# Regrouping the weight loads of a decode kernel: wo by eight heads, w2 whole, the last K ahead of the last three V, w1's last rows dealt anew

## The chip, the cores and the metric

The kernel runs on one core of one Trainium2 chip. The metric is the device time of one execution in microseconds (us). A run of a kernel is several such executions on one chip, and they are timed in rounds against the kernel before on the same chip. The time is some 1.8 us longer than the span that the profile shows.

## The reference

```python
B, D, H, Dh, F = 4, 640, 32, 192, 1536         # bf16, one new token for each of 4 sequences
xn = layernorm(x)
q  = (xn @ wq)                                 # wq: 640 x 6144, 32 heads of 192
k, v = k_cache[:, :, -2048:], v_cache[:, :, -2048:]   # a window of the 8192 cached keys
o  = softmax(q k^T / sqrt(192)) v              # a head of its own for each query head
A  = o.reshape(4, 6144) @ wo                   # wo: 6144 x 640
Bf = (silu(xn @ w1) * (xn @ w3)) @ w2          # w1, w3: 640 x 1536; w2: 1536 x 640
out = x + A + Bf
```

For each head 3 MB of K and 3 MB of V come from memory and are used once. With the weights that makes 223 MB in one execution, against little arithmetic.

## The kernel before

Nearly all loads are issued by one engine (SP) into one queue (q1, 222.96 MB), and SP issues a load when its buffer is free: for a K buffer it waited 316.2 us in all, 30 times, for the `mult` that frees it. Time inside the program is counted in slots of a quarter of a head: `add(slot, phase, function, ...)` puts a piece of work into a slot, and `NU - 6` is a slot near the end.

A head's attention: `mult` (DVE) multiplies K by the broadcast query, `adder` (PE) sums over the 192 elements, a short softmax chain follows, and `pv` (PE) multiplies by V. `ge_sum` sums a head's result into `po`. When a group of HG heads is complete, `ge_turn` scales and transposes it to `oT`, and `ge_proj` multiplies it by the group's rows of wo into `acc`.

```python
def load_k(h):
    kt = kpool.tile([P, NJ, Dh], BF16, tag="kt")            # 2 buffers; the V pool has 3
    nc.sync.dma_start(out=..., in_=k_win[:, h]...)          # 24,576 B a partition
def wo_load(hg):                                            # HG = 4: eight loads of 768 rows
    wo_t = wopool.tile([P, RPP * D], BF16, tag="wo")        # RPP = 6 rows a partition
    nc.sync.dma_start(out=wo_t[:], in_=A_wo[hg * QW:(hg + 1) * QW, :].rearrange("(p i) n -> p (i n)", i=RPP))
...
# w1, 640 rows: 512 rows as four a partition, 64 rows as half a row a partition (128 partitions),
# and the last 64 rows on three DMA engines, four partitions each
def w1_load():
    nc.sync.dma_start(out=wt[:, 0:FM], in_=w[0:KM * P, :].rearrange("(p kc) n -> p (kc n)", kc=KM))
    nc.sync.dma_start(out=wt[:, FM:FH], in_=w[KM * P:LB, :].rearrange("r (h n) -> (r h) n", h=2))
def w1_low(n):
    if n < 2:        # two loads of 12 partitions, two rows each
        nc.sync.dma_start(out=we[n * CT:n * CT + LP, :], in_=w[...].rearrange("(i e s) n -> e i (s n)", e=LE, s=2))
    elif n == 2:     # one load of 12 partitions, one row each
    ...              # and one of 12 partitions, a third of a row each
...
for h in range(H - 2, H):                                   # the end of the queue
    add(NU - 6, 0, load_v, h)
add(NU - 6, 0, w2_load, 0)                                  # w2 rows 0-3 of 12 a partition
add(NU - 6, 0, w2_load, 1)                                  # rows 4-7
add(NU - 6, 0, wo_load, NG - 2)
add(NU - 6, 0, wo_load, NG - 1)
add(NU - 6, 0, w2_load, 2)                                  # rows 8-10
add(NU - 6, 0, w2_load, 3)                                  # row 11
```

Why three engines take the last 64 rows of w1: in the packet records of before the 15 instruction fetches (16,384 B each) go round eight other DMA engines, hit seven of them twice and make the engine hit 1.4 us late each time, so the kernel before loads three of the remaining ones a little more. These three are called the low engines below; that is only a name.

## Time and profile before

| | before |
|---|---|
| time, median of 3 (range) | 525.66 us (525.56 to 526.65) |
| span of the profiled execution | 523.80 us |
| last byte of the loads lands | 520.49 |
| last matmul ends | 521.09 |
| share of the span in which the DMA engines carry loads | 99.2% |

The middle three rows divide the end of the span into three parts: what the loads set (520.49), what must run behind the last byte (0.60), and what ends the program (2.71). A change of the loads acts on the first part, a change of the order on the second. A wait of PE in mid-kernel is in none of them: before the matmuls of `adder` it waited 137.5 us in all for DVE, and the loads still fill 99.2% of the span. The landing times are read from the trace's packet records, which give start, duration and size of every packet. They name no engine: where a text below speaks of one, its packets were followed from the end of one to the start of the next. The lines of the profile itself are in the prediction.

### The profile page before, as it was taken

To read this page: it belongs to the slowest core of one execution; us is meant where nothing else is said; L and a number is where in the kernel's file an instruction comes from. 1 tells how busy PE (TensorE), PEld (TensorE's weight loads), DVE (VectorE), ACT (ScalarE), POOL (GpSimd) and SP (SyncE) were. 2 spreads that over 40 slices of the span, in tenths; PEclk is the share of its full clock that TensorE was granted. 3 is DMA by queue.
4 is the path that set the end of the run, shared out by engine and by line. 5 is a ranking of instruction groups with operands and counts; after the bars stand their busy time and mean duration, and the time that the engine had idled before them with its cause. 6 is when DMAs were issued, how large, how long until landed. Compare 5 with 4: busy or idle time off the path is not lost.

```text
span 523.8 us, 4820 instructions
## 1 busy us (share of the span) xinstructions
PE 361.8 (69%) x2336; PEld 75.9 (14%) x1643; DVE 340.9 (65%) x413; ACT 55.8 (11%) x176; POOL 5.6 (1%) x12
## 2 busy tenths in 40 slices
PE   0965866887668776667547768586686876675685
PEld 0100111121111111111111111111111111111122
DVE  3268853687656767577646877466667766667671
ACT  2111111111001110101100111001101110011111
POOL 4000000000000000000000000000000000000000
PEclk9979886898878998789997988889878898889988
DMA  9999999999999999999999999999999999999996
GB/s 389 422 443 425 433 431 432 428 433 432 430 435 428 437 418 446 424 437 426 434 434 429 432 434 429 435 427 435 425 437 434 427 437 431 430 434 425 441 418 275
DMA packets 11904, 223.26 MB, mean 426 GB/s; under 512 B 1332, under 2 KB 1608, under 8 KB 3052
## 3 DMA queue, kind: packets, MB, share of 16 engines
q1 hardware_dynamic: 11868, 222.96, 99.2%
q8 instruction: 15, 0.25, 0.2%
q14 instruction: 5, 0.04, 0.0%
q10 hardware_dynamic: 16, 0.01, 0.0%
HBM read 222.96 MB, written 0.01 MB: 426 GB/s over the span
## 4 chain that ended last, share of the span: by engine, by line
DMA 60%; PE 20%; DVE 15%; ACT 3%; issue 1%; SPq 1%
DMA kt<-in_A_k_cache_dram 44%; PE ps L288 11%; DMA w<-in_B_w_dram 11%; DVE pr L277 10%; DMA vt<-in_A_v_cache_dram 5%; PE po L361 4%; PE qps L243 3%; DVE sc L296 2%; ACT ex L324 1%; DVE z L332 1%; DMA x_sb<-in_A_x_dram 1%; PE mt L318 1%; ACT L324 0%; ACT negm L321 0%; PE mt L305 0%
## 5 line engine op out<-in xcount | busy, mean ns | idle before, releaser
L288 PE MATMUL ps<-pr,idb 128*128 128x512 bf16 x768 | 214.7, 422 | 137.6 <-DVE pr L277 137.5
L277 DVE TENSOR_TENSOR pr<-kt,qbc 128x3072 bf16<-128x3072 bf16 x128 | 223.5, 1746 | 104.0 <-DMA kt<-in_A_k_cache_dram 104.0
L296 DVE TENSOR_REDUCE sc<-ps 128x16 f32<-128x512 f32 x128 | 87.1, 681 | 2.7 <-PE ps L288 2.6
L340 PE MATMUL o_ps<-vt,z 128*8 128x384 bf16 x1024 | 60.5, 380 | 0.2 <-DVE z L332 0.2
L361 PE MATMUL po<-o_sb,sel_w 128*32 128x192 f32 x128 | 49.2, 518 | 0.6 <-ACT o_sb L343 0.6
L340 PEld LDWEIGHTS <-z 128*8 128x8 bf16 x1024 | 26.2, 95 | 98.8 <-issue 89.2
L332 DVE TENSOR_TENSOR z<-ex,mask_b 128x256 bf16<-128x256 bf16 x32 | 13.5, 423 | 38.6 <-ACT ex L324 38.6
L343 ACT COPY o_sb<-o_ps 128x384 f32<-128x384 f32 x32 | 15.3, 478 | 196.9 <-PE o_ps L340 196.9
L313 ACT ACTIVATE gneg<-gmax 1x128 f32<-1x128 f32 x32 | 9.8, 308 | 162.8 <-DVE gmax L310 162.8
L305 PEld LDWEIGHTS mt<-idf,lmax 128*1 128x1 f32 x32 | 3.2, 101 | 127.5 <-issue 125.5
L361 PEld LDWEIGHTS po<-o_sb,sel_w 128*32 128x32 f32 x128 | 13.8, 130 | 29.4 <-issue 27.9
L288 PEld LDWEIGHTS <-idb 128*128 128x128 bf16 x124 | 12.0, 97 | 39.3 <-issue 32.8
L318 PEld LDWEIGHTS mt<-ones_ff,gneg 1*128 1x128 f32 x64 | 9.6, 186 | 47.1 <-issue 43.7
L243 PE MATMUL qps<-wt,xnT 128*128 128x512 bf16 x59 | 14.9, 412 | 0.1
L318 PE MATMUL mt<-ones_ff,gneg 1*128 1x1 f32 x64 | 12.3, 259 | 0.7 <-ACT gneg L313 0.7
L321 ACT COPY negm<-mt 128x1 f32<-128x1 f32 x32 | 5.1, 159 | 70.4 <-PE mt L318 70.4
L310 DVE TENSOR_REDUCE gmax<-mt 1x4 f32<-1x128 f32 x32 | 8.8, 274 | 5.8 <-PE mt L305 5.8
L348 PEld LDWEIGHTS po<-rsum,tot_w 128*32 128x32 f32 x64 | 4.4, 108 | 51.5 <-ACT ex L324 35.4
L249 DVE CAST qbc<-qps 128x512 bf16<-128x512 f32 x6 | 3.8, 684 | 11.7 <-PE qps L243 11.7
L324 ACT ACTIVATE ex<-sc,negm 128x64 bf16<-128x64 f32 x32 | 11.1, 348 | 1.0
L305 PE MATMUL mt<-idf,lmax 128*1 128x128 f32 x32 | 10.9, 340 | 0.0
L199 PE MATMUL xnT_ps<-idb,xn 4*128 4x4 bf16 x5 | 0.4, 178 | 13.4 <-DVE xn L194 13.4
(74 smaller groups left out, 84.4 us busy)
## 6 DMA issues: line engine op xcount, KB each, us to landing
kt<-in_A_k_cache_dram SPq DMA_DIRECT2D x32, 3072.0 KB, 19.1
vt<-in_A_v_cache_dram SPq DMA_DIRECT2D x32, 3072.0 KB, 25.5
wo_t<-in_A_wo_dram SPq DMA_DIRECT2D x8, 960.0 KB, 20.7
wt<-in_A_wq_dram SPq DMA_DIRECT2D x2, 3072.0 KB
w<-in_B_w_dram SPq DMA_DIRECT2D x1, 1920.0 KB
wt<-in_A_wq_dram SPq DMA_DIRECT2D x1, 1536.0 KB, 19.5
w<-in_B_w_dram SPq DMA_DIRECT2D x1, 1536.0 KB
w<-in_B_w_dram SPq DMA_DIRECT2D x2, 640.0 KB
```

Source lines behind the costliest of these rows:

```text
L243: nc.tensor.matmul(qp[:], lhsT=xnT[:, kc].rearrange("p a b -> p (a b)"), rhs=wq_rows[kc][:, (c0 + i) * QC:(c0 + i + 1) * QC], start=(kc == ...
L277: nc.vector.tensor_tensor(out=pr[:], in0=kts[h][:, g * JQ:(g + 1) * JQ, :], in1=qbc[:, h * Dh:(h + 1) * Dh].unsqueeze(1).to_broadcast([P, ...
L288: nc.tensor.matmul(ps[:], lhsT=idb[:], rhs=pr[:, :, kk * DD:(kk + 1) * DD], start=(kk == 0), stop=(kk == NK - 1))
L296: nc.vector.tensor_reduce(out=scs[h][:, g * JQ:(g + 1) * JQ], in_=pss.pop(u)[:], axis=AX.X, op=ALU.add)
L305: nc.tensor.transpose(out=mt[0:1, 0:P], in_=chs[h][0][:], identity=idf[:])
L313: nc.scalar.activation(out=gneg[:], in_=gmax[:].unsqueeze(1).to_broadcast([1, PB, B]), func=ACTF.Copy, scale=-SCALE)
L318: nc.tensor.matmul(mt[:, P:P + 1], lhsT=gneg[:].rearrange("o p b -> o (p b)"), rhs=ones_ff[:], start=True, stop=True)
L324: nc.scalar.activation(out=ex[:], in_=scs.pop(h)[:], func=ACTF.Exp, bias=negm[:, 0:1], scale=SCALE, accum_out=rsum[:])
L332: nc.vector.tensor_tensor(out=z[:], in0=ex[:].unsqueeze(2).to_broadcast([P, NJ, B]), in1=mask_b[:].unsqueeze(1).to_broadcast([P, NJ, B]), ...
L340: nc.tensor.matmul(o_ps[c * CT:c * CT + 2 * B, :], lhsT=z[:, 2 * jj:2 * jj + 2, :], rhs=vt[:, 2 * jj:2 * jj + 2, :], start=(jj < 4), stop= ...
L343: nc.scalar.copy(out=o_sb[:], in_=o_ps[:])
L361: nc.tensor.matmul(po[sl, 0:Dh], lhsT=sel_w[:, par].rearrange("p a b -> p (a b)"), rhs=o_sb[:, par * Dh:(par + 1) * Dh].rearrange("p (r i) ...
```

## The change

The intent: fewer and larger packets (wo in four loads instead of eight, w2 in one instead of four), the attention of the last heads out of the way of the last loads (K of the last head ahead of the last three V), and a deal of w1 in which each of the 16 engines has one packet less and the three low engines more.

```diff
-    HG: int = 4,
+    HG: int = 8,
+    FG: int = 4,
...
-    wopool = ctx.enter_context(tc.tile_pool(name="wo", bufs=2))
+    wopool = ctx.enter_context(tc.tile_pool(name="wo", bufs=1))
...
     def load_k(h):
-        kt = kpool.tile([P, NJ, Dh], BF16, tag="kt")
+        kt = (kpool if h < H - 1 else vpool).tile([P, NJ, Dh], BF16, tag="kt" if h < H - 1 else "vt", name="kt")
...
-    KM, PH, LE, LI = KC - 1, P // 2, 3, 4
+    KM, LE, LI, LS = KC - 1, 3, 4, 3
+    LP, LF = LE * LI, CT + LE * LI
+    PH = D - KM * P - 2 * LP * LS        # 56 rows, so 112 half rows
...
     def ge_turn(hg):
-        nc.vector.tensor_scalar_mul(out=og[:]..., in0=po[:, 0:Dh], scalar1=rts.pop(hg)[:, 0:1])
+        nc.vector.tensor_tensor(out=og[:], in0=po_v, in1=rts.pop(hg)[:]....to_broadcast([P, RPP, HB, RW]), op=ALU.mult)
...
-        nc.sync.dma_start(out=wt[:, FM:FH], in_=w[KM * P:LB, :].rearrange("r (h n) -> (r h) n", h=2))
+        nc.sync.dma_start(out=wt[0:2 * PH, FM:], in_=B_w1[KM * P:LB, :].rearrange("r (h n) -> (r h) n", h=2))
...
     def w1_low(n):
-        if n < 2: ...                    # four loads, 12 partitions each
+        b0 = LB + n * LS * LP            # two loads, 12 partitions of three rows each
+        nc.sync.dma_start(out=ffn["w1e"][n * CT:n * CT + LP].rearrange("p s n -> p (s n)"), in_=B_w1[b0:b0 + LS * LP, :]...)
...
-    ends = {H - 2: (NU - 1, NU), H - 1: (NU + 3, NU + 4)}
+    ends = {H - 3: (NU - 1, NU), H - 2: (NU + 2, NU + 3), H - 1: (NU + 4, NU + 5)}
+    early = {H - 1: (NU - 10, -1)}
...
+    WOC = [0, RPP - 5, RPP - 2, RPP]     # RPP is 12 now: rows 0-6, 7-9, 10-11
     for h in range(H - 2, H):
         add(NU - 6, 0, load_v, h)
-    add(NU - 6, 0, w2_load, 0)           # and the other five loads shown above
...
+    add(NU - 6, 0, w2_load)
+    for i0, i1 in zip(WOC, WOC[1:]):
+        add(NU - 6, 0, wo_load, NG - 1, i0, i1)
+        add(e, 6, ge_proj, NG - 1, i0, i1, True)
+    add(e - 1, 8, ffn_out)
```

More of the change, by code (lines that the diff above doesn't have):

```diff
@@ L87 @@
     CT = 32
+    HB = HG * CT // P
     QW = HG * Dh
     RPP = QW // P
+    RW = Dh // RPP
     NU = H * GQ
@@ L95 @@
     assert JQ * DD == 512 and JQ % 2 == 0 and 2 * Dh <= 512 and 2 * N0 == D and N0 <= 512
-    assert (H * Dh) % QC == 0 and NQ % 6 == 0 and QW % P == 0 and Dh == CT * RPP and P == HG * CT and F == HG * CT * FC
-    assert 2 * H * Dh <= NJ * Dh and KBUFS == 2 and VBUFS == 3
+    assert (H * Dh) % QC == 0 and NQ % 6 == 0 and QW % P == 0 and Dh == RW * RPP and CT == HB * RW and P == FG * CT and F == FG * CT * FC
+    assert 2 * H * Dh <= NJ * Dh and KBUFS == 2 and VBUFS == 3 and HB * (Dh + 1) <= 512 and H // HG > 1
     nc.at_finalize(keep_loaded_weights)
@@ L127, in load_k, with load_v, wo_load @@
         kts[h] = kt
-    def load_v(h, n=1):
-        vt = vpool.tile([P, NJ, Dh], BF16, tag="vt")
-        for j in range(0, NJ, NJ // n):
-            nc.sync.dma_start(out=vt[:, j:j + NJ // n].rearrange("q j d -> q (j d)"),
-                              in_=v_win[:, h].rearrange("b (p j) d -> p b j d", p=PB)[:, :, j:j + NJ // n].rearrange("p b j d -> p b (j d)"))
-        vts[h] = vt
-    def wo_load(hg):
-        wo_t = wopool.tile([P, RPP * D], BF16, tag="wo")
-        nc.sync.dma_start(out=wo_t[:], in_=A_wo[hg * QW:(hg + 1) * QW, :].rearrange("(p i) n -> p (i n)", i=RPP))
-        wos[hg] = wo_t
+    def load_v(h):
+        vt = (vpool if h < H - 1 else kpool).tile([P, NJ, Dh], BF16, tag="vt" if h < H - 1 else "kt", name="vt")
+        nc.sync.dma_start(out=vt[:].rearrange("q j d -> q (j d)"),
+                          in_=v_win[:, h].rearrange("b (p j) d -> p b (j d)", p=PB))
+        vts[h] = vt
+    def wo_load(hg, i0=0, i1=RPP):
+        if i0 == 0:
+            wos[hg] = wopool.tile([P, RPP * D], BF16, tag="wo", name="wo_t")
+        nc.sync.dma_start(out=wos[hg][:, i0 * D:i1 * D],
+                          in_=A_wo[hg * QW:(hg + 1) * QW, :].rearrange("(p i) n -> p i n", i=RPP)[:, i0:i1, :].rearrange("p i n -> p (i n)"))
     x_sb = const.tile([B, D], BF16, name="x_sb")
@@ L201 @@
     nc.vector.tensor_copy(out=xnT[:], in_=xnT_ps[:].unsqueeze(2).to_broadcast([P, KC, PB, B]))
-    KM, PH, LE, LI = KC - 1, P // 2, 3, 4
-    LP, LF, LB = LE * LI, CT + LE * LI, KM * P + PH
-    assert D - LB == 5 * LP + LI and F % LE == 0
+    KM, LE, LI, LS = KC - 1, 3, 4, 3
+    LP, LF = LE * LI, CT + LE * LI
+    PH = D - KM * P - 2 * LP * LS
+    LB = KM * P + PH
+    assert 0 < PH <= P // 2
     xm = ppool.tile([B, 2, PH, 2], BF16, tag="pr", name="xm")
@@ L212 @@
         nc.vector.tensor_copy(out=xm[:, i, :, i], in_=xn[:, KM * P:LB])
-    xe = ppool.tile([B, 3 + LE, LF], BF16, tag="pr", name="xe")
+    xe = ppool.tile([B, LS, LF], BF16, tag="pr", name="xe")
     nc.gpsimd.memset(xe[:], 0.0)
     for g in range(2):
-        b0 = LB + g * 2 * LP
-        nc.vector.tensor_copy(out=xe[:, 0:2, g * CT:g * CT + LP].rearrange("b s (e i) -> b s e i", i=LI),
-                              in_=xn[:, b0:b0 + 2 * LP].rearrange("b (i e s) -> b s e i", e=LE, s=2))
-    nc.vector.tensor_copy(out=xe[:, 2, 0:LP].rearrange("b (e i) -> b e i", i=LI),
-                          in_=xn[:, LB + 4 * LP:LB + 5 * LP].rearrange("b (i e) -> b e i", e=LE))
-    for e in range(LE):
-        nc.vector.tensor_copy(out=xe[:, 3 + e, CT + e * LI:CT + (e + 1) * LI], in_=xn[:, LB + 5 * LP:D])
-    NX = KM + 2
-    xw_ps = ps_t.tile([P, NX + 3 + LE, B], BF16, tag="t", name="xw_ps")
+        b0 = LB + g * LS * LP
+        nc.vector.tensor_copy(out=xe[:, :, g * CT:g * CT + LP].rearrange("b s (e i) -> b s e i", i=LI),
+                              in_=xn[:, b0:b0 + LS * LP].rearrange("b (i e s) -> b s e i", e=LE, s=LS))
+    xw_ps = ps_t.tile([P, KM + 2 + LS, B], BF16, tag="t", name="xw_ps")
     for kc in range(KM):
@@ L227, with weights @@
     for i in range(2):
-        nc.tensor.transpose(out=xw_ps[:, KM + i, :], in_=xm[:, i].rearrange("b r h -> b (r h)"), identity=idb[0:B, 0:B])
-    for i in range(3 + LE):
-        nc.tensor.transpose(out=xw_ps[0:LF, NX + i, :], in_=xe[:, i, :], identity=idb[0:B, 0:B])
-    xw = const.tile([P, NX, NREP, B], BF16, name="xw")
-    nc.vector.tensor_copy(out=xw[:], in_=xw_ps[:, 0:NX, :].unsqueeze(2).to_broadcast([P, NX, NREP, B]))
-    xl = const.tile([LF, 3 + LE, NREP, B], BF16, name="xl")
-    nc.vector.tensor_copy(out=xl[:], in_=xw_ps[0:LF, NX:, :].unsqueeze(2).to_broadcast([LF, 3 + LE, NREP, B]))
+        nc.tensor.transpose(out=xw_ps[0:2 * PH, KM + i, :], in_=xm[:, i].rearrange("b r h -> b (r h)"), identity=idb[0:B, 0:B])
+    for i in range(LS):
+        nc.tensor.transpose(out=xw_ps[0:LF, KM + 2 + i, :], in_=xe[:, i, :], identity=idb[0:B, 0:B])
+    def weights(name, p, c0, c1):
+        t = const.tile([p, c1 - c0, NREP, B], BF16, name=name)
+        nc.vector.tensor_copy(out=t[:], in_=xw_ps[0:p, c0:c1, :].unsqueeze(2).to_broadcast([p, c1 - c0, NREP, B]))
+        return t
+    xw = weights("xw", P, 0, KM)
+    xh = weights("xh", 2 * PH, KM, KM + 2)
+    xl = weights("xl", LF, KM + 2, KM + 2 + LS)
     qbc = const.tile([P, H * Dh], BF16, name="qbc")
@@ L268, in acc_add @@
             acc_half(i, lhsT, rhs, last=last)
-    po = ps_po.tile([P, Dh + 1], FP32, name="po")
+    po = ps_po.tile([P, HB * (Dh + 1)], FP32, name="po")
+    po_v = po[:, 0:HB * Dh].rearrange("p (i x r) -> p i x r", x=HB, r=RW)
     def x_add(i):
@@ L346, in ge_tot @@
     def ge_tot(h):
-        sl = slice((h % HG) * CT, (h % HG + 1) * CT)
-        nc.tensor.matmul(po[sl, Dh:Dh + 1], lhsT=tot_w[:].rearrange("p a b -> p (a b)"), rhs=rsums.pop(h)[:],
-                         start=True, stop=True)
+        blk, x = (h % HG) // HB, h % HB
+        nc.tensor.matmul(po[blk * CT:(blk + 1) * CT, HB * Dh + x:HB * Dh + x + 1], lhsT=tot_w[:].rearrange("p a b -> p (a b)"),
+                         rhs=rsums.pop(h)[:], start=True, stop=True)
         chs.pop(h)
     def ge_rec(hg):
-        rt = small.tile([P, 1], FP32, tag="rt", bufs=2, name="rt")
@@ L354, in ge_rec @@
-        nc.vector.reciprocal(out=rt[:], in_=po[:, Dh:Dh + 1])
+        rt = small.tile([P, HB], FP32, tag="rt", bufs=2, name="rt")
+        nc.vector.reciprocal(out=rt[:], in_=po[:, HB * Dh:HB * (Dh + 1)])
         rts[hg] = rt
     def ge_sum(h):
-        sl = slice((h % HG) * CT, (h % HG + 1) * CT)
+        blk, x = (h % HG) // HB, h % HB
         o_sb = o_sbs.pop(h)
         for par in range(2):
-            nc.tensor.matmul(po[sl, 0:Dh], lhsT=sel_w[:, par].rearrange("p a b -> p (a b)"),
+            nc.tensor.matmul(po_v[blk * CT:(blk + 1) * CT, :, x, :], lhsT=sel_w[:, par].rearrange("p a b -> p (a b)"),
@@ L362, in ge_sum @@
                              rhs=o_sb[:, par * Dh:(par + 1) * Dh].rearrange("p (r i) -> p i r", i=RPP), start=(par == 0), stop=(par == 1))
     def ge_turn(hg):
-        og = small.tile([P, RPP, CT], BF16, tag="og", bufs=1, name="og")
-        nc.vector.tensor_scalar_mul(out=og[:].rearrange("p i r -> p (i r)"), in0=po[:, 0:Dh],
-                                    scalar1=rts.pop(hg)[:, 0:1])
+        og = small.tile([P, RPP, HB, RW], BF16, tag="og", bufs=1, name="og")
+        nc.vector.tensor_tensor(out=og[:], in0=po_v, in1=rts.pop(hg)[:].unsqueeze(1).unsqueeze(3).to_broadcast([P, RPP, HB, RW]),
+                                op=ALU.mult)
@@ L368, in ge_turn, with ge_proj @@
         oT = small.tile([P, RPP, CT], BF16, tag="oT", bufs=2, name="oT")
-        nc.vector.transpose(out=oT[:].rearrange("p i r -> p (i r)"), in_=og[:].rearrange("p i r -> p (i r)"))
+        nc.vector.transpose(out=oT[:].rearrange("p i r -> p (i r)"), in_=og[:].rearrange("p i x r -> p (i x r)"))
         oTs[hg] = oT
-    def ge_proj(hg, i0, i1):
+    def ge_proj(hg, i0, i1, last=False):
         oT, wo_t = oTs[hg], wos[hg]
         for i in range(i0, i1):
-            acc_add(oT[:, i, 0:B], wo_t[:, i * D:(i + 1) * D])
@@ L378 @@
-    FW = F // HG
+            acc_add(oT[:, i, 0:B], wo_t[:, i * D:(i + 1) * D], last=last and i == RPP - 1)
+    FW = F // FG
     sT = const.tile([P, FW], FP32, name="sT")
@@ L382 @@
     ffn = {}
-    FM, FH = KM * F, KM * F + F // 2
+    FM = KM * F
     def w1_load():
-        w = B_w1
-        wt = fpool.tile([P, FH + F], BF16, tag="w", name="w1")
-        we = wopool.tile([LF, 2 * F], BF16, tag="wo", name="w1e")
+        wt = fpool.tile([P, FM + F // 2], BF16, tag="w", name="w1")
+        we = wopool.tile([LF, LS, F], BF16, tag="wo", name="w1e")
         nc.gpsimd.memset(we[:], 0.0)
-        nc.gpsimd.memset(wt[0:LF, FH:], 0.0)
-        nc.sync.dma_start(out=wt[:, 0:FM], in_=w[0:KM * P, :].rearrange("(p kc) n -> p (kc n)", kc=KM))
-        nc.sync.dma_start(out=wt[:, FM:FH], in_=w[KM * P:LB, :].rearrange("r (h n) -> (r h) n", h=2))
+        nc.sync.dma_start(out=wt[:, 0:FM], in_=B_w1[0:KM * P, :].rearrange("(p kc) n -> p (kc n)", kc=KM))
+        nc.sync.dma_start(out=wt[0:2 * PH, FM:], in_=B_w1[KM * P:LB, :].rearrange("r (h n) -> (r h) n", h=2))
         ffn["w1"], ffn["w1e"] = wt, we
     def w1_low(n):
-        w, wt, we = B_w1, ffn["w1"], ffn["w1e"]
-        if n < 2:
-            b0 = LB + n * 2 * LP
-            nc.sync.dma_start(out=we[n * CT:n * CT + LP, :],
-                              in_=w[b0:b0 + 2 * LP, :].rearrange("(i e s) n -> e i (s n)", e=LE, s=2))
-        elif n == 2:
-            nc.sync.dma_start(out=wt[0:LP, FH:FH + F], in_=w[LB + 4 * LP:LB + 5 * LP, :].rearrange("(i e) n -> e i n", e=LE))
-        else:
-            nc.sync.dma_start(out=wt[CT:LF, FH:FH + F // LE], in_=w[LB + 5 * LP:D, :].rearrange("i (e n) -> e i n", e=LE))
+        b0 = LB + n * LS * LP
+        nc.sync.dma_start(out=ffn["w1e"][n * CT:n * CT + LP].rearrange("p s n -> p (s n)"),
+                          in_=B_w1[b0:b0 + LS * LP, :].rearrange("(i e s) n -> e i (s n)", e=LE, s=LS))
     def w1_in():
@@ L409, in w1_in, with mm @@
         ps = ffn["ps"] = ps_t.tile([P, FW], FP32, tag="t", name="f_ps")
-        def mm(w, lhsT, rhs, c0=0, start=False, stop=False):
-            nc.tensor.matmul(ps[w * CT:(w + 1) * CT, c0:c0 + rhs.shape[1]], lhsT=lhsT.rearrange("p a b -> p (a b)"), rhs=rhs,
-                             start=start, stop=stop)
+        def mm(w, lhsT, rhs, start=False, stop=False):
+            nc.tensor.matmul(ps[w * CT:(w + 1) * CT, :], lhsT=lhsT.rearrange("p a b -> p (a b)"), rhs=rhs, start=start, stop=stop)
         def main(kc):
-            for w in range(HG):
+            for w in range(FG):
                 mm(w, xw[:, kc], wt[:, kc * F + w * FW:kc * F + (w + 1) * FW], start=(kc == 0), stop=(kc == KM - 1))
         main(0)
-        for w in range(HG):
+        for w in range(FG):
             c0 = FM + (w % 2) * FW
-            mm(w, xw[:, KM + w // 2], wt[:, c0:c0 + FW])
-        for i in range(2):
-            for w in range(HG):
-                mm(w, xl[:, i], we[:, i * F + w * FW:i * F + (w + 1) * FW])
-        for w in range(HG):
-            mm(w, xl[:, 2], wt[0:LF, FH + w * FW:FH + (w + 1) * FW])
-        FE = F // LE
-        for e in range(LE):
-            for w in range(HG):
-                c0, c1 = max(e * FE, w * FW), min((e + 1) * FE, (w + 1) * FW)
-                if c0 < c1:
-                    mm(w, xl[:, 3 + e], wt[0:LF, FH + c0 - e * FE:FH + c1 - e * FE], c0 - w * FW)
+            mm(w, xh[:, w // 2], wt[0:2 * PH, c0:c0 + FW])
+        for i in range(LS):
+            for w in range(FG):
+                mm(w, xl[:, i], we[:, i, w * FW:(w + 1) * FW])
         for kc in range(1, KM):
@@ L444, in w3_in @@
         for kc in range(KC):
-            for w in range(HG):
+            for w in range(FG):
                 nc.tensor.matmul(ffn["ps"][w * CT:(w + 1) * CT, :], lhsT=xnT[:, kc].rearrange("p a b -> p (a b)")[:, 0:CT],
@@ L458, with w2_load, ffn_out @@
     w2_v = B_w2.rearrange("(p c) n -> p c n", c=FC)
-    W2C = [0, FC - 8, FC - 4, FC - 1, FC]
-    def w2_load(i):
-        if i == 0:
-            ffn["w2"] = fpool.tile([P, FC, D], BF16, tag="w", name="w2")
-        c0, c1 = W2C[i:i + 2]
-        nc.sync.dma_start(out=ffn["w2"][:, c0:c1, :].rearrange("p c n -> p (c n)"),
-                          in_=w2_v[:, c0:c1, :].rearrange("p c n -> p (c n)"))
-    def ffn_out(i):
-        for c in range(*W2C[i:i + 2]):
-            acc_add(hT[:, c, 0:B], ffn["w2"][:, c, :], last=(c == FC - 1))
+    def w2_load():
+        wt = fpool.tile([P, FC, D], BF16, tag="w", name="w2")
+        nc.sync.dma_start(out=wt[:].rearrange("p c n -> p (c n)"), in_=w2_v.rearrange("p c n -> p (c n)"))
+        ffn["w2"] = wt
+    def ffn_out():
+        for c in range(FC):
+            acc_add(hT[:, c, 0:B], ffn["w2"][:, c, :])
     sched = defaultdict(list)
@@ L482 @@
         if h >= KBUFS:
-            add((h - KBUFS + 1) * GQ, 0, load_k, h)
+            add(*early.get(h, ((h - KBUFS + 1) * GQ, 0)), load_k, h)
         if h < H - 2:
@@ L503 @@
     e = ends[H - 1][1] + 1
-    for hg in range(NG - 2):
+    for hg in range(NG - 1):
         a = ((hg + 1) * HG - 1) * GQ + L + 3
-        add(hg * HG * GQ + 8, 0, wo_load, hg)
-        add(a, 6, ge_proj, hg, 0, RPP // 2)
-        add(a + 1, 6, ge_proj, hg, RPP // 2, RPP)
+        add(hg * HG * GQ + 17, 0, wo_load, hg)
+        for n in range(4):
+            add(a + n, 6, ge_proj, hg, n * RPP // 4, (n + 1) * RPP // 4)
     add(3, 0, w1_load)
-    for n in range(4):
-        add(4 + 2 * n, 1, w1_low, n)
+    for n in range(2):
+        add(5 + 3 * n, 1, w1_low, n)
     add(13, 7, w1_in)
@@ L518 @@
     add(17, 6, x_add, 1)
+    WOC = [0, RPP - 5, RPP - 2, RPP]
     for h in range(H - 2, H):
         add(NU - 6, 0, load_v, h)
-    add(NU - 6, 0, w2_load, 0)
-    add(NU - 6, 0, w2_load, 1)
-    add(NU - 6, 0, wo_load, NG - 2)
-    add(NU - 6, 0, wo_load, NG - 1)
-    add(NU - 6, 0, w2_load, 2)
-    add(NU - 6, 0, w2_load, 3)
-    add(e - 1, 8, ffn_out, 0)
-    add(e - 1, 8, ffn_out, 1)
-    add(e - 1, 8, ge_proj, NG - 2, 0, RPP)
-    add(e, 6, ge_proj, NG - 1, 0, RPP)
-    add(e, 7, ffn_out, 2)
-    add(e, 7, ffn_out, 3)
+    add(NU - 6, 0, w2_load)
[3 more added lines that the diff above has]
+    add(e - 1, 8, ffn_out)
     for s in sorted(sched):
```

## The prediction

> **What bounds the kernel now.** I read the page first: the slices and the DMA queues.
>
> ```profile
> span 523.8 us, 4820 instructions
> ...
> PE   0965866887668776667547768586686876675685
> ...
> DVE  3268853687656767577646877466667766667671
> ...
> DMA  9999999999999999999999999999999999999996
> GB/s 389 422 443 425 433 431 432 428 433 432 430 435 428 437 418 446 424 437 426 434 434 429 432 434 429 435 427 435 425 437 434 427 437 431 430 434 425 441 418 275
> ...
> q1 hardware_dynamic: 11868, 222.96, 99.2%
> q8 instruction: 15, 0.25, 0.2%
> ```
>
> The reader is to see a transfer row of nines to the last slice, while no compute engine is full. The 16 DMA engines carry loads for 99.2% of the span. So the time is: a short head (the first packet starts at 1.0 us), the work of the slowest DMA engine, and what must run after the last byte. A compute engine that waits in mid-kernel costs nothing, as long as the queue holds work. It does: the last K load is issued at 478.0 and is not needed by the DMA engines before 486, a lead of 8 us.
>
> Second, the stretches of the end.
>
> ```profile
> core 0: us, PE busy (x) PEld busy (x) DVE busy (x) ACT busy (x) POOL busy (x), PEclk, DMA share, GB/s
> ...
> 450.00:507.00 57.00, 41.16 (x291) 9.37 (x211) 39.56 (x47) 5.54 (x20) 0.00 (x0) 0.91 1.00 432
> 507.00:517.00 10.00, 7.18 (x64) 2.32 (x53) 3.16 (x7) 1.86 (x6) 0.00 (x0) 0.83 0.99 415
> 517.00:520.50 3.50, 2.83 (x44) 1.69 (x40) 0.80 (x2) 0.00 (x0) 0.00 (x0) 1.00 0.66 267
> 520.50:523.80 3.30, 0.59 (x8) 0.25 (x4) 0.48 (x1) 0.42 (x1) 0.00 (x0) 0.97 0.00 2
> ```
>
> The DMA share falls to 0.66 between 517.0 and 520.5: some DMA engines have finished and others not. 0.34 of 3.5 us is 1.2 us of the whole set lost. Third, the timeline of the end.
>
> ```profile
> 489.68 7.64 SPq L465 DMA_DIRECT2D w<-in_B_w_dram  x2
> ...
> 518.65 0.38 DVE L369 STREAM_TRANSPOSE oT<-og 128x192 bf16<-128x192 bf16 x1
> 519.08 0.76 PEld L264 LDWEIGHTS <-oT 128*4 128x4 bf16 x12 [0.70 <-DVE oT L369]
> 519.21 0.98 PE L264 MATMUL acc<-wo_t,oT 128*4 128x320 bf16 x12 [0.47 <-DMA wo_t<-in_A_wo_dram]
> 519.89 0.09 PEld L264 LDWEIGHTS <-hT 128*4 128x4 bf16 x1
> 520.38 0.71 PE L264 MATMUL acc<-w,hT 128*4 128x320 bf16 x8 [0.19 <-DMA w<-in_B_w_dram]
> ```
>
> The last attention result is turned at 519.03, just before the last wo lands (0.47 us of waiting), then w2's last pieces are waited for. Both chains, attention and loads, end almost together; the loads end last. Matmuls end at 521.09, and the copies, the store and its receipt take the rest, 2.7 us.
>
> The trace's packet records (start, duration, size) give the price list. From start to start on one DMA engine: 24,576 B 908 ns, 7,680 B 287, 5,120 B 193, 3,840 B 146, 1,536 B 61, 1,280 B 52, and 6 for the 4-byte semaphore packet that closes a transfer. Fitted, that is 4.6 ns a packet plus 0.03677 ns a byte. The last semaphore packet ends at 520.49, and the first matmul that needs it starts 0.31 us later.
>
> The spread has two causes in the same records. The 12-partition pieces of w1 put 2.5 us on three engines alone. And each of the 15 instruction fetches of the q8 line makes one engine late by 1.4 us; they go round eight engines, so seven were hit twice (2.8 us). The times at which one V load closes on the 16 engines, near 500 us, lie over 3.25 us: seven at 2.88 to 3.25 (mostly the twice-hit), the three w1 engines at 2.36, 2.46 and 3.02, six at 1.4 or less.
>
> [...]
>
> **The change, part by part.**
> wo in groups of eight: per DMA engine, before 8 transfers of 8 packets of 7,680 B, 64 × 287 = 18.37 us. After, three transfers of 8 × 15,360 B (569 by the fit), 13.67 us, and the last in three pieces, 8 × (334 + 146 + 99) = 4.63: 18.30 us. Saving 0.07. Matmuls stay at 96. The scaling and the transpose are twice as wide (a 384-wide transpose took 578 ns in the ffn, against 378), four times instead of eight; off the bound.
> w2: before 16 × 193 + 8 × 146 + 8 × 52 = 4.67 us, after 8 × 569 = 4.55. Saving 0.12.
> Semaphores: 12 transfers of wo and w2 become 7, saving 0.03.
> w1: the evenly spread piece falls from 8 packets to 7, saving 0.06 on all. The three low engines go from 8 × 230 + 4 × 117 + 4 × 42.5 + 4 × 6 = 2.50 us to 8 × 343 + 2 × 6 = 2.76, so +0.26 on these three.
> Sum: the common work −0.28 us, the three low ones −0.02. The late twice-hit ones stand at 3.25 − 0.28 = 2.97, the latest low one at 3.02 − 0.02 = 3.00. The deal evens them. The last byte then comes at 520.49 − 0.25 = about 520.24. The number of fetches should stay 15[...].
> The end: w2 is now before wo, and the last piece (rows 10 and 11 of 12) needs 4 matmuls instead of 2. Twelve took 0.98, one 0.298, so 0.062 each: +0.12 us. The middle piece lands 0.8 us earlier, and its 6 matmuls (0.61) fit there. Net: −0.25 + 0.12 = −0.13 us.
> Last K first: mult of the last K can start near 489.7 instead of 497.0. Before, the last V's matmuls waited for the softmax until 513.3; now they wait for V itself, all engines through at 511.2, so 511.5. Then 1.5 to 2.7 us, copy 0.5, sums 1.5, scaling and transpose about 1.1 (estimated from the widths): oT at 516.2 to 517.4, before the first wo piece at about 518.5. This moves the attention chain some 2 us off the end. It was waiting for a load anyway, so it buys safety, not time.
>
> **The rivals.**
> (1) A slow tensor clock in the tail. The granted clock drops to half for 3.4 us at a time; PE now has 24 w2 and 24 wo matmuls behind the last V. If the drop falls on 518 to 521.5, matmuls at double pitch add about 1 us: 526.6. For it: one of the three runs of before took 526.65. Against: before has the same exposure, and now has less slack in attention than after.
> (2) A gap in the queue: larger wo loads come just after K and delay the next, and the last V loads must wait for buffers freed by pv. If SP were held over 8 us, the time would rise by what is over, perhaps 2 to 3 us: 528. Against: V30 waits for pv of head 28, which ended near 481, and the DMA engines want V30 at 493. Also w1's last piece is issued earlier, so w3 waits less. I give it 5%.
> (3) The late engines are not those I think: if the low ones are hit by a fetch as well, or the attention chain really was the limit, the gain could be 0.3 to 1 us: 524.7 to 525.3. For it: turning and landing were only 0.2 us apart. Against: the last waits all name loads.
>
> **Range and chances.** 525.66 − 0.13 = 525.5 us. Runs of before spread over 1.1 us, rival 3 gives the lower edge, rival 1 the upper: 524.8 to 526.4. Two per cent is 10.5 us, and no rival reaches it[...].
>
> **What would show it.** Right: queue share still 99%, transfers closing 3 us apart at the end, the last wo piece landing near 520.2 with no wait of PE on oT, and 4 matmuls then. The wait of og on the sums moves well before 518. Wrong: a dip in a mid-kernel slice, oT after 518.5, more than 15 fetches, or a last byte outside 519.9 to 520.6.

No term of the sum went with them: it is −0.25 + 0.12 = −0.13 us, and 525.66 − 0.13 is about 525.5. What the trace of before shows: 432 GB/s from 450 to 507 us; 1,324 semaphore packets, which are 82 transfers by 16 engines and 4 by 3; 15 fetches, 32 us apart in the mean. The granted clock of rival 1 is at 0.5 there in 25 stretches of 3.41 us and 4 of 6.83.

## The result, and the profile after

The kernel after took 525.90 us, median of six (525.65 to 527.30); the kernel before in the same rounds 525.71 (525.56 to 526.79). The ratio is 1.0006 with a 95% interval of 0.9990 to 1.0022: the same. (A ratio here is the mean time of one kernel's fast runs over that of the other's of the same rounds, so not quite the ratio of the medians.) In these few executions both kernels take either about 525.6 to 525.9 or 526.6 to 527.3. A difference of 0.2 us can't be told from zero by timing; where parts of a microsecond are in question below, they come from the packet and instruction records of one profiled execution of each kernel, and I say how far two profiles of one kernel lie apart.

The page of the kernel after:

```profile
span 524.1 us, 4775 instructions
...
PE   0965867574685786863867676765776876685786
...
DMA  9999999999999999999999999999999999999996
GB/s 391 422 441 413 437 427 432 428 435 439 425 435 430 440 428 431 429 430 439 427 432 431 435 427 435 433 431 431 430 435 430 435 428 433 437 424 438 428 427 263
...
q1 hardware_dynamic: 11102, 222.96, 99.2%
q8 instruction: 15, 0.25, 0.2%
```

The row of nines is still there, the same 222.96 MB go in 766 packets fewer (11,868 before), the queue's share is the same 99.2%, and the fetches are 15 as they were. So the change did what it was meant to do with the packets and was not followed by a gap in the queue; yet the span is 0.3 us longer. A slice to look at again is the fourth: 413 GB/s, against 425 before. It covers 39.3 to 52.4 us, in which w1 is loaded.

The stretches of the end, same columns as before:

```profile
507.00:517.00 10.00, 7.12 (x84) 3.17 (x86) 1.73 (x4) 1.84 (x6) 0.00 (x0) 0.97 0.98 417
517.00:520.50 3.50, 3.50 (x36) 1.89 (x32) 0.00 (x0) 0.00 (x0) 0.00 (x0) 0.61 0.65 267
520.50:524.00 3.50, 0.78 (x12) 0.33 (x8) 0.48 (x1) 0.42 (x1) 0.00 (x0) 1.00 0.00 1
```

Between 517.0 and 520.5 the DMA share is 0.65, where it was 0.66: the engines end as unevenly as before. And PE is now busy for all of these 3.50 us at a granted clock of 0.61 (before: 2.83 us at 1.00).

The timeline of the end (start, duration, engine, line, operation; in brackets the idle time before it and what ended that):

```profile
515.23 0.56 DVE L372 TENSOR_TENSOR og<-po,rt 128x384 bf16<-128x384 f32 x1 [3.81 <-PE po L367]
515.82 0.58 DVE L375 STREAM_TRANSPOSE oT<-og 128x384 bf16<-128x384 bf16 x1
516.18 3.27 PE L269 MATMUL acc<-w,hT 128*4 128x320 bf16 x24 [0.99 <-DMA w<-in_B_w_dram]
519.24 2.04 PE L269 MATMUL acc<-wo_t,oT 128*4 128x320 bf16 x24
```

The attention result is turned at 516.40, 2.6 us earlier than before (519.03). In this execution PE waits for nothing behind 516.18, neither for attention nor for a load: the 24 matmuls of wo follow the 24 of w2 at once, and they carry no bracket.

A second profile of the same kernel (r_after, below) differs here, and the two should be read together. The clock is full, and PE waits for both parts of wo:

```profile
517.00:520.50 3.50, 2.58 (x38) 1.49 (x33) 0.66 (x2) 0.00 (x0) 0.00 (x0) 1.00 0.69 282
...
516.31 1.79 PE L269 MATMUL acc<-w,hT 128*4 128x320 bf16 x24
518.98 1.74 PE L269 MATMUL acc<-wo_t,oT 128*4 128x320 bf16 x20 [0.87 <-DMA wo_t<-in_A_wo_dram]
520.93 0.44 PE L269 MATMUL acc<-wo_t,oT 128*4 128x320 bf16 x4 [0.22 <-DMA wo_t<-in_A_wo_dram]
```

The result is turned at 517.70 there, and at 518.12 in the second profile of before.

The three parts of the end, from the records of the executions that were profiled (us; "last byte" is the end of the last load's closing packet):

| kernel | last byte | matmuls end | span |
|---|---|---|---|
| before | 520.49 | 521.09 | 523.80 |
| before, profiled again (r_before) | 520.47 | 521.08 | 523.80 |
| after | 520.47 | 521.28 | 524.11 |
| after, profiled again (r_after) | 520.61 | 521.37 | 524.19 |

So, after against before: the last byte comes 0.02 us earlier (0.12 later in the second profile), where 0.25 earlier was predicted. The work behind it takes 0.81 instead of 0.60, and the rest of the program 2.83 instead of 2.71. Part of that last one lies in the end of the program: from the end of the output's packets to the end of the span it takes 1.16 before and 1.27 after. There SP goes through its final waits one by one, some 62 ns each, and the wait that ends as the output lands stands at another place in that list (it is the last one in before, and two follow it in after). The sum is −0.02 + 0.21 + 0.12 = +0.31 us.

### The profile page after: what moved, and what is told of

Its sections match the earlier page's. It is cut to its first block, busy times and chain, and to the rows that moved or that the text cites. A ratio compares the mean times of both kernels' runs of the same rounds, so it can differ in the third digit from the quotient of the medians.

```text
span 524.1 us, 4775 instructions
## 1 busy us (share of the span) xinstructions
PE 356.9 (68%) x2327; PEld 75.5 (14%) x1633; DVE 339.3 (65%) x398; ACT 55.9 (11%) x176; POOL 5.4 (1%) x11
## 3 DMA queue, kind: packets, MB, share of 16 engines
q1 hardware_dynamic: 11102, 222.96, 99.2%
HBM read 222.96 MB, written 0.01 MB: 425 GB/s over the span
## 4 chain that ended last, share of the span: by engine, by line
DMA 60%; DVE 19%; PE 18%; ACT 2%; issue 1%; SPq 0%
DMA kt<-in_A_k_cache_dram 52%; DVE pr L283 13%; PE ps L294 9%; DMA w<-in_B_w_dram 7%; PE po L367 3%; PE qps L248 3%; DVE sc L302 3%; DVE z L338 1%; DMA x_sb<-in_A_x_dram 1%; ACT ex L330 1%; PE acc L269 1%; PE mt L324 1%; ACT L330 0%; PE mt L311 0%; ACT negm L327 0%
## 5 line engine op out<-in xcount | busy, mean ns | idle before, releaser
L294 PE MATMUL ps<-pr,idb 128*128 128x512 bf16 x768 | 212.2, 418 | 145.9 <-DVE pr L283 145.8
L346 PE MATMUL o_ps<-vt,z 128*8 128x384 bf16 x1024 | 55.5, 361 | 0.8 <-DMA vt<-in_A_v_cache_dram 0.8
L346 PEld LDWEIGHTS <-z 128*8 128x8 bf16 x1024 | 24.9, 92 | 101.4 <-issue 91.4
```

Source lines behind the costliest of these rows:

```text
L294: nc.tensor.matmul(ps[:], lhsT=idb[:], rhs=pr[:, :, kk * DD:(kk + 1) * DD], start=(kk == 0), stop=(kk == NK - 1))
L346: nc.tensor.matmul(o_ps[c * CT:c * CT + 2 * B, :], lhsT=z[:, 2 * jj:2 * jj + 2, :], rhs=vt[:, 2 * jj:2 * jj + 2, :], start=(jj < 4), stop= ...
```

## The experiments

My first theory was that the new deal of w1 had lost what the larger packets had won: the packets right behind w1's small load of 112 partitions are slow. In the kernel before, the first packet of the next K load takes 912 ns on every engine. In after it takes 1,112 to 1,227 ns on all 16. The 112 partitions give each engine seven packets of 1,536 B, the 128 of before eight. The rivals were the slow tensor clock in the tail, the early K, which changes when buffers come free, and low engines that are hit by fetches as well.

### The kernels again

The kernel before, unchanged, for one look:

> The kernel before, unchanged, to see how far one profiled execution repeats. My theory (the time is the finish of the latest DMA engine plus the work after the last byte): last byte at 520.3 to 520.6 us, the first packets of the third K load take 912 ns, span 523.6 to 524.0. Rival (the 0.2 us between the two kernels is chance, from which engines the instruction fetches hit): the last byte moves by 0.3 us or more against the first profile.

It took 525.59 us with a span of 523.80, and its records (table above) agree with the first profile within 0.02 us. The first K packets behind w1's small load took 912 ns on at least 12 of 16 engines; a few took up to 1,312.

The kernel after, unchanged, on another chip, timed:

> The changed kernel again, for its spread and a second profile. My theory now (the small load of w1, 1,536 B a packet, is followed by a slow stretch of the third K load, of a length that differs from run to run, 0.03 to 1.4 us an engine in the six profiles so far): the slow stretch is there again, most runs 525.6 to 526.1, one or two of six at 526.7 to 527.6. Rival (each kernel has its own fixed stall): 0.29 us an engine again, and the profile repeats to 0.05 us.

It took 526.00 (525.75 to 527.77), ratio 1.0004 [0.9992, 1.0017]. The slow first packets came again, 1,055 to 1,291 ns. The last byte was 0.13 later than in the other profile of this kernel, so that is how far two profiles of after lie apart.

### Only the new deal of w1, and everything but it

The kernel before with w1's new deal alone (e_w1new), and the kernel after with the old one (e_w1old):

```diff
 # e_w1new, against before (the matmuls that use w1 go with it)
-    KM, PH, LE, LI = KC - 1, P // 2, 3, 4
+    KM, LE, LI, LS = KC - 1, 3, 4, 3
...
-        nc.sync.dma_start(out=wt[:, FM:FH], in_=w[KM * P:LB, :]...)                 # 128 partitions
+        nc.sync.dma_start(out=wt[0:2 * PH, FM:], in_=B_w1[KM * P:LB, :]...)         # 112 partitions
...
-    for n in range(4):
-        add(4 + 2 * n, 1, w1_low, n)
+    for n in range(2):
+        add(5 + 3 * n, 1, w1_low, n)
```

> Before with only w1's new deal. My theory (the load of 112 partitions makes the next packet of every DMA engine take 1,150 ns instead of 912, so 0.24 us is lost on all): the first packets of the third K load take about 1,150 ns; against before the common engines -0.06 + 0.24 = +0.18 us, the three low ones +0.26 - 0.07 + 0.24 = +0.43; the low ones become the latest, last byte 520.6 to 520.8, time +0.2 to +0.3 us. Rival (the slow packets of that profile were chance): packets at 912 ns, last byte 520.4 to 520.5, time 0.0.

> After with before's deal of w1 and all else of the change. My theory: no slow packets; last byte at 520.49 - 0.07 - 0.12 - 0.03 = about 520.27 us; the end with two pairs of matmuls instead of one, so 525.6 (-0.3 against after, -0.1 against before). Rival (w1's deal does nothing, the stall belongs to the order of the rest): the slow packets stay and the time stays at 525.9.

Measured: e_w1new 525.98 (525.90 to 527.52), ratio 1.0008 [0.9993, 1.0022]; e_w1old 525.90 (525.60 to 526.99), ratio 1.0002 [0.9990, 1.0015]. By the clock both are the same as before. The records tell more. In e_w1old the last byte lands at 520.14, 0.35 us earlier than before; in e_w1new at 520.57, 0.08 later. One line of the DMA view of 44 to 56 us shows the stretch behind w1's small loads, in before, after and e_w1old in this order:

```profile
DMA packets 419, 5.27 MB, mean 439 GB/s; under 512 B 51, under 2 KB 179, under 8 KB 191
```
```profile
DMA packets 395, 5.11 MB, mean 426 GB/s; under 512 B 51, under 2 KB 163, under 8 KB 163
```
```profile
DMA packets 419, 5.26 MB, mean 438 GB/s; under 512 B 51, under 2 KB 179, under 8 KB 191
```

The two with the old deal move 439 and 438 GB/s, the one with the new deal 426. So in after the stretch is slow with the new deal of w1 and not with the old one, while the larger wo and the early K stay. The deal alone, put into before, does not show it at that size: in e_w1new the first packets behind the small load took 939 to 996 ns, and not the 1,150 expected, nor the 912 of the rival. To size the effect I summed, over the large packets (24,576 B) that start from 44 to 57 us, what each takes above 912 ns, and divided by the 16 engines. The result is in the table at the end of this part.

But e_w1old doesn't end earlier by those 0.35 us. Its span is 523.84, that of before, because 0.14 goes into a longer tail (0.74 from last byte to last matmul, 0.60 before) and 0.24 into the end of the program (1.40 from the output's packets to the end, as four waits follow the output's). Its timeline:

```profile
515.87 1.79 PE L267 MATMUL acc<-w,hT 128*4 128x320 bf16 x24 [0.99 <-DMA w<-in_B_w_dram]
518.53 1.71 PE L267 MATMUL acc<-wo_t,oT 128*4 128x320 bf16 x20 [0.87 <-DMA wo_t<-in_A_wo_dram]
520.45 0.44 PE L267 MATMUL acc<-wo_t,oT 128*4 128x320 bf16 x4 [0.21 <-DMA wo_t<-in_A_wo_dram]
```

Here the tensor clock was full: 24 matmuls took 1.79 us, not 3.27, and PE waited for both pieces of wo. It still took 0.74 us from the last byte to the last matmul. The second profile of after says the same of the same kernel: full clock, and 0.76. The slow clock in the first profile of after (0.81) therefore cost some 0.05 us: rival 1 of the prediction came true in part, and is not the answer. (e_noearly below has 0.81 at full clock, so even the 0.05 isn't clear.)

### Without the early K

The kernel after with K and V of the last heads in the buffers, the order and the slots of before (e_noearly):

```diff
-        kt = (kpool if h < H - 1 else vpool).tile([P, NJ, Dh], BF16, tag="kt" if h < H - 1 else "vt", name="kt")
+        kt = kpool.tile([P, NJ, Dh], BF16, tag="kt", name="kt")
...
-    ends = {H - 3: (NU - 1, NU), H - 2: (NU + 2, NU + 3), H - 1: (NU + 4, NU + 5)}
-    early = {H - 1: (NU - 10, -1)}
+    ends = {H - 2: (NU - 1, NU), H - 1: (NU + 3, NU + 4)}
+    early = {}
```

> After without the early last K (loads in the order of before, and the last three heads' steps at before's slots). My theory: the attention chain goes back by some 2 us, so that the transpose of the last group ends at 518.8 to 519.2 us and the 24 wo matmuls all come behind it: end of matmuls 519.1 + 1.7 to 2.0 (full clock) = 520.9 to 521.2, so the time changes by -0.1 to +0.2 us; the early K buys slack and no time. Rival (the early K is what kept the change from being slower): +0.8 us or more.

It took 526.16 (525.83 to 527.37), ratio 1.0010 [0.9997, 1.0023]. The profiled execution was one of the long ones (527.03, span 525.24).

```profile
518.94 0.58 DVE L375 STREAM_TRANSPOSE oT<-og 128x384 bf16<-128x384 bf16 x1
...
520.08 1.71 PE L269 MATMUL acc<-wo_t,oT 128*4 128x320 bf16 x20 [0.86 <-DMA wo_t<-in_A_wo_dram]
```

Without the early K the result is turned at 519.52, which is 3.1 and 1.8 us later than in the two profiles of after, and some 1.1 us of that is this execution's lateness. Even so PE waits 0.86 us for wo behind it. Last byte to last matmul is 0.81, as in after. So the early K buys slack and no time, as predicted. This execution is about 1.1 us late in its loads, and that too is seen in one place: the first 16 packets of the K load behind w1's small load took 1,161 to 1,296 ns, and those after them, of K and of the V behind it, mostly 1,000 to 1,050 until about 55 us, where they take 912 in before. Summed from 44 to 57 us that is 1.42 us on every engine.

### The small load of w1 elsewhere

The kernel after with the 112-partition load issued behind the third K load instead of ahead of it (e_midlate):

```diff
-        nc.sync.dma_start(out=wt[0:2 * PH, FM:], in_=B_w1[KM * P:LB, :].rearrange("r (h n) -> (r h) n", h=2))
...
+    def w1_half():
+        nc.sync.dma_start(out=ffn["w1"][0:2 * PH, FM:], in_=B_w1[KM * P:LB, :].rearrange("r (h n) -> (r h) n", h=2))
...
     add(3, 0, w1_load)
+    add(4, 0, w1_half)
```

> After with w1's small load issued behind the third K load instead of ahead of it. My theory (the slow stretch follows the small load): the third K load takes 912 ns a packet throughout, and slow packets, if any, are those of the second V load, which comes after the small load. Rival (the third K load, or this time of the run, is slow by itself): packets over 1,000 ns stay in the third K load or at 45.5 to 47 us. Time 525.6 to 526.0 either way.

It took 526.13 (525.95 to 527.76), ratio 1.0007 [0.9995, 1.0020]. The windows of 44 to 52 and 52 to 58 us (columns as in the prediction):

```profile
44.00:52.00 8.00, 3.93 (x20) 0.72 (x7) 6.66 (x8) 2.19 (x5) 0.00 (x0) 1.00 1.04 445
52.00:58.00 6.00, 5.79 (x45) 0.96 (x34) 3.62 (x5) 0.48 (x1) 0.00 (x0) 0.72 0.98 382
```

The K load that was slow now takes 912 ns a packet (but for one beside a fetch), and the packets that start from 52.8 to 54.4 us, beside and behind the moved load, take mostly 1,130 to 1,315: 382 GB/s, against 441 in the same window of before. The slow packets follow the load.

### Eight engines for w1's last rows, in two ways

If eight engines, which I took to be the ones left alone by the fetches (called the eight low engines), took an eighth each of w1's last 128 rows, the fetched engines would have less to carry and all could end together. Two forms of it (both on after): in e_k8 one load to 128 partitions, in eight groups of 16 neighbours; in e_k8own two loads to 32 partitions each, in eight groups of four, at the offsets 0 and 32.

```diff
 # e_k8: 128 partitions, one row each, slowest dimension 8
+        nc.sync.dma_start(out=ffn["w1"][:, FM:], in_=B_w1[KM * P:D, :].rearrange("(i e) n -> e i n", e=8))
```
```diff
 # e_k8own: two loads of 32 partitions, two rows each, slowest dimension 8
+        nc.sync.dma_start(out=ffn["w1e"][n * 32:(n + 1) * 32].rearrange("p s n -> p (s n)"),
+                          in_=B_w1[b0:b0 + 64, :].rearrange("(i e s) n -> e i (s n)", e=8, s=2))
```

In the kernels named "tail" wo's last piece is one row instead of two as well:

```diff
-    WOC = [0, RPP - 5, RPP - 2, RPP]
+    WOC = [0, RPP - 5, RPP - 1, RPP]
```

> After with the last 128 rows of w1 in one load, one row a partition, on eight DMA engines (rows dealt so that the slowest dimension of the source is 8). No small load is left. My theory: the twice-fetched engines lose 7 x 61 = 0.43 us and the stretch of 0.24; the eight others get 16 x 117 = 1.88 us, which is less than the 2.8 of two fetches. Last byte 520.47 - 0.43 - 0.24 - 0.1 = about 519.7 us, no slow stretch, no run at 526.7 or above; end of matmuls 520.5, time 525.1 to 525.3 (-0.5 against before). Rival A (the latest engines are not the fetched ones): last byte within 0.2 of 520.47. Rival B (the slow stretch belongs to the third K load): slow packets and some runs above 526.7 stay.

> The same with wo's last pieces as rows 0-6, 7-10 and 11 instead of 0-6, 7-9 and 10-11. My theory: one pair of matmuls (0.136 us at full clock) less behind the last byte: 525.0 to 525.2, if PE is not backed up. Rival (PE is backed up behind w2 and wo, not waiting for the last piece): no difference to the run before.

> After with the last 128 rows of w1 in two loads of 32 partitions on eight DMA engines, four partitions an engine, two rows of 6,144 B in all per packet; same engines and bytes as the run with eight engines before, other partitions. My theory[...]: packets of 6,144 B at 234 ns, the K and V loads beside them at 912, no slow stretch; common engines -0.43 - 0.29 us against after, the eight +1.84; last byte 519.4 to 519.8, time 525.0 to 525.3, no run above 526.5. Rival (any load on eight of sixteen engines slows the rest): the 52 to 58 us stretch at 300 GB/s or less again, time 527.5 to 529.

> The same with wo's last pieces as rows 0-6, 7-10 and 11. My theory: one pair of matmuls less behind the last byte, -0.07 to -0.14 us against the run before it: 524.9 to 525.2. Rival (PE is backed up by then): 0.0.

e_k8 took 528.76 (528.55 to 529.14), ratio 1.0053 [1.0041, 1.0065]; with the shorter tail 528.96, ratio 1.0054. e_k8own took 526.66 (526.55 to 526.87), ratio 1.0017 [1.0003, 1.0030]; with the shorter tail 526.51 (526.44 to 526.78), ratio 1.0015. None is faster than before, and the shorter tail is worth nothing that the runs can tell. The windows of 52 to 58 us of before, e_k8 and e_k8own:

```profile
52.00:58.00 6.00, 5.08 (x42) 0.80 (x33) 4.54 (x6) 0.48 (x1) 0.00 (x0) 0.72 1.03 441
```
```profile
52.00:58.00 6.00, 6.00 (x46) 1.08 (x36) 3.94 (x5) 0.48 (x1) 0.00 (x0) 0.72 1.03 266
```
```profile
52.00:58.00 6.00, 5.62 (x44) 1.14 (x34) 5.18 (x6) 0.48 (x1) 0.00 (x0) 0.72 0.98 414
```

The reader is to see that in e_k8 the DMA engines are all busy (1.03) and move only 266 GB/s. The records say how: its own packets of 3,072 B take 242 ns in the median (117 by the prediction's fit), and the V packets that run beside them on the other engines take up to 2,120 ns instead of 912. In e_k8own eight engines carry the same bytes, one half at this place and the other at 68 us; the large packets stay at 912 ns, and its own of 6,144 B take 234 in the median. The two differ in how the partitions are grouped, in the packet's size and in the number of loads. In before, packets of 3,072 and of 6,144 B on the three low engines leave the large packets beside them at 912 ns, which speaks against the size. In e_k8 the load's packets begin to take over 200 ns at 53.3 us, when four or five an engine (about 13 KB) have gone, and in e_k8own four an engine (24.6 KB) pass without that, which speaks against the halved amount. That leaves the grouping of the partitions as my guess. It was not shown: no run changes it alone, and no record of the trace names a partition.

e_k8own failed for another reason. Thirteen engines had finished by 519.67, as I had expected of all, but three finished at 521.01 to 521.31. Followed from packet to packet these three are low engines, and they end up to 3.0 us behind others of the eight, about what two fetches of 1.4 us cost. So I take it that some of the eight low engines are hit by fetches too; the assumption that the fetched ones are all among the others fell. The choice of just three engines in the kernel before is a good fit to that.

Does the same deal cost as much without the rest of the change? The kernel before with it (e_b_k8own; the edit is the same, on before):

> Before with only this deal of w1. My theory: last byte 520.49 - 0.49 - 0.05 = about 519.95, but in before the attention chain ends at 519.0 and wo's and w2's 20 matmuls behind it need 1.7 us, so the end of matmuls is held near 520.7: time 525.2 to 525.5. Rival (the loads alone set the end): 525.1.

526.82 (526.75 to 527.05), ratio 1.0021 [1.0008, 1.0033], with its matmuls ending at 522.03:

```profile
520.13 0.98 PE L256 MATMUL acc<-wo_t,oT 128*4 128x320 bf16 x12 [1.31 <-DMA wo_t<-in_A_wo_dram]
...
521.32 0.71 PE L256 MATMUL acc<-w,hT 128*4 128x320 bf16 x8 [0.22 <-DMA w<-in_B_w_dram]
```

PE waits for the late loads, 1.31 and 0.22 us. The loss is that of e_k8own, with or without the rest of the change.

A side result: the 25 executions of these five kernels lie within 0.6 us of each other for each kernel. None is a long one, whereas each kernel with six or more timed executions and three low engines has one or more, 1.2 to 2.0 us above its fastest. I took it that the long ones come from the same place, the packets behind the small load, as they did in the profile of e_noearly.

### An attempt to beat both

e_half is the kernel after, with w1's first 576 rows in one load of 128 partitions of nine half rows each (13,824 B a partition), no small load behind it, the old low rows on three engines, and wo's last piece of one row. Its own theory: no slow packets, hence also no long executions.

```diff
-        nc.sync.dma_start(out=wt[:, 0:FM], in_=B_w1[0:KM * P, :].rearrange("(p kc) n -> p (kc n)", kc=KM))
-        nc.sync.dma_start(out=wt[0:2 * PH, FM:], in_=B_w1[KM * P:LB, :].rearrange("r (h n) -> (r h) n", h=2))
+        nc.sync.dma_start(out=wt[:, 0:FH], in_=w[0:LB, :].rearrange("(m r) n -> m (r n)", r=NH).rearrange("m (q k) -> (m q) k", q=2))
...
-    WOC = [0, RPP - 5, RPP - 2, RPP]
+    WOC = [0, RPP - 5, RPP - 1, RPP]
```

> A version meant to beat both: after with before's rows for the three low engines (its 12-partition loads), but without the small load: 576 rows of w1 in one load of 128 partitions, nine half rows (13,824 B) each, with masked x weights for the two halves; and wo's last pieces as rows 0-6, 7-10, 11. My theory ([...]25 runs of the five kernels with eight engines, which have no small load, had no such outlier): third K load at 912 ns a packet, last byte 520.14 - 0.04 - 0.05 = about 520.05 us (against 520.14 in after with the old deal), 525.4 to 525.6, all runs within 0.4 us of each other. Rival (outliers are chance and belong to any kernel): one or two of six at 526.6 or above, median 525.7 to 525.9.

It took 526.39 (525.79 to 527.77), ratio 1.0014 [1.0000, 1.0028]: no gain. The profiled execution (525.79) has its last byte at 520.31, 0.18 before that of the kernel before, and a span of 524.00. Two of six executions were long (527.29 and 527.77). So the long executions do not come from the small load alone, and my theory of them fell; their cause is open. No kernel of this study beats the one before.

### The stretch behind w1's small loads, all kernels

"Extra" is the sum described above, per engine; 0.03 or 0.04 of it is in most runs a single packet beside a fetch of 8 KB.

| kernel | small load | extra, us | last byte |
|---|---|---|---|
| before / r_before | 128 partitions | 0.03 / 0.08 | 520.49 / 520.47 |
| e_w1old | 128 partitions | 0.06 | 520.14 |
| e_half | none | 0.14 | 520.31 |
| e_w1new | 112 partitions | 0.10 | 520.57 |
| after / r_after | 112 partitions | 0.29 / 0.35 | 520.47 / 520.61 |
| e_midlate | 112 partitions, moved | 0.38 | 520.82 |
| e_noearly (a long execution) | 112 partitions | 1.42 | 521.61 |
| e_k8 / e_k8_tail | one load, eight groups of 16 | 1.46 / 1.45 | 523.53 / 523.69 |
| e_k8own / e_k8own_tail / e_b_k8own | two loads, eight groups of 4 | 0.01 / 0.00 / 0.07 | 521.31 / 521.25 / 521.34 |

The large effects separate cleanly (0.29 and more only with the load of 112 partitions or with the eight groups of 16). The small ones don't: e_half has 0.14 with no small load, e_w1new 0.10 with one. What the load of 112 costs thus differs between kernels and executions, from 0.10 to 0.38 us apart from the long one, and why is open.

## Why the prediction was right or wrong

525.90 lies in the range of 524.8 to 526.4, 0.4 above the number. Point by point:

- **What bounds the kernel**: right. Queue share 99.2% in both, no dip in mid-kernel, 15 fetches in both.
- **Packet prices**: right. Packets of 15,360 B took 573 to 575 ns from end to end, with 569 from start to start; 8,960 B 338; 3,840 B 149; 2,560 B 102; 9,216 B 347. These last four are from end to end too, 3 to 4 ns above the start-to-start prices that the prediction worked out (334, 146, 99, 343).
- **wo, w2 and semaphores, −0.22 us**: right in direction. e_w1old, in which these act without the deal of w1, had its last byte 0.35 earlier. One profile doesn't settle whether the other 0.13 is real.
- **w1, the step that failed**: "the evenly spread piece falls from 8 packets to 7, saving 0.06 on all". The prediction priced the load by its own packets alone. The packets behind the load of 112 partitions became slow, by 0.29 and 0.35 us an engine in the two profiles of after, of which 0.04 is one packet beside a fetch. So on all engines the term was a loss of some 0.2 us and not a gain of 0.06, and the last byte, put at "520.49 − 0.25", came at 520.47 and 520.61, the second just outside the 519.9 to 520.6 that the prediction had named. With the old deal (e_w1old) it came at 520.14. The deal alone (e_w1new) cost only 0.10, so its price is not one fixed number. The mechanism of the sum was right; what it lacked is that a load can make the packets behind it slow. That this comes from the partitions was not shown; I had fitted prices to loads of 128 and 12 partitions only.
- **The three low engines as the latest** (3.00 against 2.97): right in order. Followed from packet to packet, one of the three closes last in both profiles of after, at 520.47 against 520.35 for the latest other engine, and at 520.61 against 520.53. That low engines have little to spare was seen in e_k8own, where three of eight came 1.3 to 1.6 us behind all others.
- **The tail, +0.12 us**: a little too small. From last byte to last matmul it was 0.74 in e_w1old and 0.76 in r_after at full clock, against 0.60: +0.14 to +0.16 by the order of the loads. It was 0.81 in after with the slow clock.
- **Last K first**: right in the main. oT at 516.40 (predicted 516.2 to 517.4) in one profile and at 517.70 in the other, both before the first wo. It gives slack, and no time that the runs can tell (e_noearly).
- **Scaling and transpose, about 1.1 us**: right, 0.56 + 0.58.
- **Rival 1, the slow clock**: it came in one of two profiles of after (0.61 in 517.0 to 520.5, and 1.00 in r_after) and cost some 0.05, not 1, because PE at full clock waits for loads in this stretch (0.87 and 0.22 us in r_after). **Rival 2, a gap in the queue**: did not come. **Rival 3**: not as stated, since on the three low engines of after no 16 KB fetch is seen. With eight low engines three came late as if hit (e_k8own), so relieving the others bought nothing there.
- **Not foreseen**: the end of the program, +0.12 in after and +0.24 in e_w1old, by the place of the output's wait among the last waits of SP.

Why so large a rearrangement moves so little is then plain. What the larger packets could win was 0.2 to 0.35 us of 525, and it was given back in three places: the new deal of w1, the longer tail and the final waits.

## What to carry to other kernels

Here the DMA engines carry loads for 99.2% of the span, and what merging transfers could win was the fixed cost, 4.6 ns a packet by the fit and 6 ns a transfer. In such a case work out that sum before rebuilding a schedule for it. When a load is dealt out to engines in an unusual number of partitions, look in the packet records at the packets beside and behind it and not only at its own: here a load of 0.17 MB made the loads behind it 0.1 to 0.4 us longer, and 1.4 in one long execution. And follow a gain through to the end of the span, since 0.35 us at the last byte was gone by the last wait.
